# A recurrent attention block with a gated feed-forward network: late values of segments 58 to 61 kept in DRAM from step 1, an eighth early gate/up pair, two down loads in step 63

## The chip, the core and the metric

One core of one Trainium2 chip runs the whole program. Its engines run their own instruction streams side by side: TensorE (PE; its weight loads are listed as PEld), VectorE (DVE), ScalarE (ACT), GpSimd (POOL) and SyncE (SP), which here mostly issues DMAs. They wait for each other by semaphores. The metric is the device time of one execution in microseconds (us); the time of the kernel before is the median of three runs. Besides there is one profiled execution with a trace of every instruction.

## The reference

All inputs are bf16: 2048 rows of width 640, 32 heads of 128, 64 segments of 32 rows, a memory of 8 rows, and a feed-forward width of 1728.

```python
def _A_ref(x, mem0, Wq, Wk, Wv, Wo, seg_len):
    ...
    mem = mem0
    for s in range(n_seg):
        xs = x[:, s * seg_len:(s + 1) * seg_len, :].copy()
        h = jnp.concatenate([mem, xs], axis=1)
        q = jnp.einsum('btd,dhe->bhte', h, Wq)
        ...
        scores = jnp.where(mask[None, None], scores, -1000000000.0)
        p = _softmax(scores, axis=-1)
        o = jnp.einsum('bhqk,bhke->bhqe', p, v)
        o = jnp.einsum('bhte,hed->btd', o, Wo)
        mem = o[:, :M, :].copy()
        outs.append(o[:, M:, :])
...
h = x + _A_ref(_layernorm(x, axis=-1), A_mem0, A_Wq, A_Wk, A_Wv, A_Wo, A_seg_len)
h2 = h + _B_ref(_layernorm(h, axis=-1), B_W_gate, B_W_up, B_W_down)
```

`_B_ref` is relu(x Wgate) times (x Wup), times Wdown. The first eight output rows of a segment are the memory of the next, so the 64 segments form a chain.

## The kernel before

**Steps.** Step s (0 to 63) handles the memory and the first 24 rows of segment s: K, Q and V projections (`project`, L387 and L414), scores (L510), the memory rows' product with the values (`pv_mem`, L564), the output projection (`wo_split` L629, `wo_pass` L612), and from that the memory rows of the next segment (`to_act_split`, L656 and L658), with which step s+1 begins. The product for the other rows of segment s-1 (`pv_x`, L707) runs inside step s, and reads merged values from VM, which SP copies there.

**Late rows.** The last eight rows of a segment don't depend on the memory. Those of four segments are projected together, 32 rows at a time: `act_e[p]` holds them, and `extra_units` gives three steps of each group of four one of the K, Q and V products (40 matmuls of 512 columns), cut in three parts (`filler(0)` to `filler(2)`) that stand between the parts of the recurrence in PE's order. Results go to Ke, Qe and Ve, two buffers each; those of buffer 1 are parts of `ends`. Step 1 has no such unit.

**Early products.** Near the end some of these places are used otherwise. The late K and Q of segments 54 to 61 are made before step 1 and kept in DRAM (`next_d`). The units freed so compute gate/up pairs of the first 512 rows of the feed-forward part (`early_product`, steps 50, 51, 54, 55, 58, 59 and 60, L913), whose inputs lie in the unused halves of Ke, Qe and Ve; results go to `hx_d` in DRAM. NE = 7 counts them. Step 56 still projects the values of segments 58 to 61, after which the feed-forward input in buffer 0 is overwritten by the saved K and Q.

**Fills.** `fill_of(s)` says how many extra weight loads or halved matmuls K, Q and V of step s are given. They change no result: a matmul that could reuse the loaded weights loads them again, or a matmul of 512 columns is made as two of 256.

**Feed-forward part.** In step 63 and behind it, `gate_up(0, j)` computes the remaining pairs of block 0, the first four with 32-column groups (L913), the others full width (L1023), the last as a tail from Wt (L1036); `down_pair` follows (L1325), then blocks 1 to 3. Weights are loaded into the space of the projection weights: `load_piece` takes the next of the pieces of Wg and Wu, `load_down(n)` three row chunks of Wd once the K weights are no longer used.

**Order.** Every operation is added to one list. Each engine takes its operations in the order of the list, and waits are derived from the named keys that operations read and write. DMAs on SP are issued in that order too, so a DMA that waits holds those behind it.

Of the kernel before, what the change touches and what calls it, by code (L numbers as in the profile page):

```python
# [5 lines left out]
BF16 = mybir.dt.bfloat16  # L6
# [21 lines left out]
class _Graph:  # L28
# [10 lines left out]
    def add(self, eng, fn, r=(), w=(), dma=False):  # L39
        if eng == "pool" and not dma:  # L40
            r, w = tuple(r) + (("pool",),), tuple(w) + (("pool",),)
        op = _Op(eng, fn, tuple(r), tuple(w), dma)
        self.ops.append(op)
        return op
# [133 lines left out]
def build_kernel(nc, A_x, A_mem0, A_Wq, A_Wk, A_Wv, A_Wo, A_seg_len, B_W_gate, B_W_up, B_W_down, out):  # L178
    _, S, D = A_x.shape
    M = A_mem0.shape[1]  # L180
    _, H, Dh = A_Wq.shape
# [17 lines left out]
    xn2_d = nc.dram_tensor("xn2_d", [128, DC, 2 * TB], BF16)  # L199
    attn_d = nc.dram_tensor("attn_d", [S, 4, DC * 32], BF16)  # L200
    ends_d = nc.dram_tensor("ends_d", [128, 64 * H + 8 * VW], BF16)
    NE = 7
    next_d = [nc.dram_tensor(f"next{i}_d", [128, 32 * H], BF16) for i in range(4)]
    hx_d = nc.dram_tensor("hx_d", [128, NE, TB], BF16)

    es = ExitStack()
# [78 lines left out]
    def ap(t, off, dims, p0=0, n=128):  # L285
        if isinstance(t, _Part):
            t, off = t.whole, t.off + off
        row = 1
        for s in t.shape[1:]:
            row *= s  # L290
        return bass.AP(t, p0 * row + off, [[row, n]] + dims)
# [59 lines left out]
    def dma(dst, src, r=(), w=(), eng="sp"):  # L351
        add(eng, lambda e: e.dma_start(dst, src), r=r, w=w, dma=True)  # L352
# [123 lines left out]
    def chunks_of(flat):  # L476
        return flat.rearrange("p (c t) -> p c t", t=128)

    def place(s):
        if s < 2 or s >= NSEG - 2:  # L480
            return 1, s % 4
        return (s - 2) // 4 % 2, (s - 2) % 4
# [106 lines left out]
    def flip_ox(s, halves=(0, 1)):  # L589
        p = (s + 1) % 2  # L590
        for kh in halves:
            add("dve", lambda v, kh=kh: v.transpose(ap(oT[p], 160 * kh + M, [[320, 4], [40, 4], [1, 32]]),  # L592
                                                       ap(tox, 128 * kh, [[256, 4], [1, 4], [4, 32]])),
                r=[("ox", kh, t) for t in range(2)], w=[("oT", p, "x", kh)])
# [337 lines left out]
        j = EARLY_STEPS.index(s)  # L932
        dma(chunks_of(t[:, :]), src[:, 128 * j:128 * j + 128].rearrange("(c p) f -> p c f", p=128), w=[k])

    EARLY_STEPS = (NSEG - 14, NSEG - 13, NSEG - 10, NSEG - 9, NSEG - 6, NSEG - 5, NSEG - 4)

    def early_product(s):
        n, hp = EARLY_STEPS.index(s), 1 - place(s)[0]
# [20 lines left out]
    def extra_units(s):  # L959
        p, r = 1 - place(s)[0], place(s)[1]  # L960
        if s == NSEG - 3:
            p = 1 - place(NSEG - 1)[0]
            j = 0
            a, ks = act_e[p], [("acte", p)]
        elif 2 <= s < NSEG - 3 and r < 3:
            j = (1, 0, 2)[r]
            a, ks = act_e[p], [("acte", p)]
            if s in EARLY_STEPS:
                return early_product(s)
        else:  # L970
            return None, None

        def part(n):
            for c, halves in PARTS[n]:
                project(a, ks, j, halves, [BQ[i] for i in halves], (c,))

        def evac():
            for i in range(2):
                if j == 2:
                    to_v(BQ[i], Ve[p], i, ("Ve", p), "act")  # L980
                else:
                    to_tok(BQ[i], 2 + i, "act")
            for i in range(2):
                if s == NSEG - 3:
                    flip(2 + i, Qe[p], i, [("Qe", p, i)])
                elif j < 2:
                    flip(2 + i, (Qe, Ke)[j][p], i, [(("Qe", "Ke")[j], p, i)])
        return part, evac

    EARLY = tuple(range(15, 47, 4))  # L990

# [128 lines left out]
    FILL = (56, 39, 7, 52)  # L1120

    def fill_of(s):
        n = {1: 31, 2: 8, 50: 0, 51: 25, 54: 0, 55: 25, 57: 39, 58: 0, 59: 27, 60: 40, 61: 39, 62: 50, 63: 0}.get(s, FILL[s % 4])
        alone = min(n // 4, 3)
        rest = n - 4 * alone
        return [k < 3 - alone for k in range(3)], [2 * ((rest // 2 + k) // 4) + (k == 0 and rest % 2) for k in range(4)]

    for s in range(1, NSEG):
# [11 lines left out]
        def filler(n):  # L1140
            if units:
                units(n)
            if woe:
                woe_pass(BQ[0], WPARTS[n])
        if s > 0:
            a, ks = pass_act(s)
            held, parts = fill_of(s)
            if s in (NSEG - 14, NSEG - 13, NSEG - 10, NSEG - 9, NSEG - 5, NSEG - 4):
                early_weights(s, 1)
            elif s in (NSEG - 12, NSEG - 8):  # L1150
                q = 1 - place(s)[0]
                for n in range(2):
                    dma((ends[:, 1024 * n:1024 * n + 1024] if q else (Ke, Qe)[n][0][:].rearrange("p h t -> p (h t)")),
                        next_d[2 * q + n][:, :], r=[("next", 2 * q + n)] + [("next", 3, i) for i in range(2) if q * n],
                        w=[(("Ke", "Qe")[n], q, i) for i in range(2)])
                add("pool", lambda p, q=q: p.memset(ap(Ve[q], Dh, [[VW, 8], [1, VW - Dh]]), 1.0),
                    w=[("Ve1", q), ("Ve", q, 0), ("Ve", q, 1)])
            elif s == NSEG - 3:
                for n in range(2):
                    dma(ends[:, 1024 * n:1024 * n + 1024], ends_d[:, 1024 * n:1024 * n + 1024], r=[("ends",)],  # L1160
                        w=END_KEYS[2 * n:2 * n + 2])
            elif s == 1:
                dma(ends_d[:, :], ends[:, :], r=END_KEYS, w=[("ends",)])
                far_save(0)
                far_save(1)
# [27 lines left out]
            if not last:  # L1193
                for i in range(2):
                    project(a, ks, 0, (i,), ((P0, P1)[i],), *WAYS[i], held=i == 1 and held[1], parts=parts[2 + i])
                    to_tok((P0, P1)[i], 2 + i, "act")
                    flip(2 + i, Qo, i, [("Qo", i)])
                    if i == 0:
                        norm_x_late(0)
                        flip_ox(s - 1, (0,))  # L1200
            else:
                norm_x_late(0)
                flip_ox(s - 1, (0,))
            if s == NSEG - 2:
                for n, (lo, hi) in enumerate(((0, 1), (1, 2), (2, 3), (3, DC))):
                    dma(xn2T[0][:, lo:hi, :], xn2_d[:, lo:hi, 0:TB], r=[("xn2_d", u) for u in range(4)] + [("Wdone", 0)],
                        w=[("xn2", 0, n)])
# [56 lines left out]
        if s in (NSEG - 15, NSEG - 11, NSEG - 7):  # L1264
            early_rows(1 - place(s + 1)[0], 0, 2)
            early_rows(1 - place(s + 1)[0], 4, DC)
            if s == NSEG - 7:
                early_weights(s + 1, 1)
        elif s in (NSEG - 14, NSEG - 10, NSEG - 6, NSEG - 5):
            early_weights(s + 1, 0)  # L1270
        norm_mem(s, 1)
        flip_mem(s, 1)
# [4 lines left out]
                w=[("Qo", i) for i in range(2)])  # L1277
        if s > 0 and not woe and s != NSEG - 3:
            late_o(s - 1)
        if s % 4 == 1 and ln:  # L1280
            ln1_back(nb, chunks_of(at[:, :]), [("at",)], "pool")
        mask_x(s)
        if e2c is not None:
# [8 lines left out]
        if s >= 1:  # L1292
            rows_split(P3, P1, wtok, ("wtok",))
            store_attn(wtok, ("wtok",), M, 32 * (s - 1), RID)
        filler(2)
        if woe:
            for n in ((s - 2, s - 1) if s == NSEG - 2 else (s - 1,)):
                late_o(n)
# [79 lines left out]
            down_store(b, u + q, o[q])  # L1378


    def load_down(n):
        lo, hi = 3 * n, min(3 * n + 3, FC - 1)
        r = [("Wdone", 1)]
        dma(Wd[:, lo:hi, :], B_W_down[128 * lo:128 * hi, :].rearrange("(j p) d -> p j d", p=128), r=r, w=[("Wd", n)])
        if n == 4:
            for q in range(2):
                dma(Wd[FR * q:FR * q + FR, FC - 1, :], B_W_down[FM:F, :], r=r, w=[("Wd", 5 + q)])

    def load_rows(b, r):
        dma(h_rows[b][:, :, :], h_d[TB * b:TB * b + TB, :].rearrange("(u p) d -> p u d", p=128),  # L1390
            r=[("h_d", 4 * b + u) for u in range(4)] + r, w=[("h", b, u) for u in range(4)])
# [18 lines left out]
        load_piece(("Wdone", 0))  # L1410
    rows(P3, s % 2, s - 1)
    gate_up(0, NE + 1)
    for n in range(2):
        load_down(n)
    pv_x(s, P0)
    norm_x(P0)
    norm_x_late(P0)
# [21 lines left out]
    for b in range(NBLK):  # L1439
        if 0 < b < NBLK - 1:  # L1440
            for u in range(4):
                ln2_load(4 * (b + 1) + u)
        for j in range(FC):
            p = j - NE if b == 0 else j
            if b or p > 3:
                gate_up(b, j)
            if b == 0 and p == 5:
                load_rows(0, [("Wdone", 1), ("hT", 0, j)])
            if b == 0 and p in (5, 6):
                load_piece(("hT", 0, j - 1))  # L1450
                load_piece(("hT", 0, j - 1))
            if 0 < b < NBLK - 1:
                fronts, backs = (1, 3, 5, 7), (3, 5, 7, 9)
                if p in fronts:
                    ln2_front(4 * (b + 1) + fronts.index(p))
                if p in backs:
                    ln2_back(4 * (b + 1) + backs.index(p), None)
        if b == 0:
            load_rows(1, [("Wdone", 2), ("hT", 0, FC - 1)])
        assert not pieces  # L1460
        for n in range(2):
            down_pair(b, n)
# [63 lines left out]
```

## Time and profile before

| what | value |
|---|---|
| median of three runs | 980.47 us (979.86 to 980.51) |
| profiled execution | 980.59 us, its span 978.9 us |
| PE busy | 955.6 us (98%), 26159 matmuls |
| PE weight loads | 537.1 us (55%), 24953 |
| VectorE busy | 726.3 us (74%) |
| ScalarE busy | 522.5 us (53%) |
| GpSimd busy | 187.4 us (19%) |
| DMA | 85.74 MB, mean 88 GB/s |

A timeline row gives the start in us, the length in us, the engine, the source line, the operation, the tile written and the tiles read, shapes, a count where rows of one kind were merged, and in brackets how long the engine had been idle before and what released it. PE's matmuls overlap, so a row's length is not its cost: that is read from the distance of starts. The row of a stage (us from A to B) gives busy time and count for each engine, the granted PE clock, the busy share of the DMA engines and GB/s.

### The profile page before, as it was taken

To read this page: it belongs to the slowest core of one execution; us is meant where nothing else is said; L and a number is where in the kernel's file an instruction comes from. 1 tells how busy PE (TensorE), PEld (TensorE's weight loads), DVE (VectorE), ACT (ScalarE), POOL (GpSimd) and SP (SyncE) were. 2 spreads that over 40 slices of the span, in tenths; PEclk is the share of its full clock that TensorE was granted. 3 is DMA by queue.
4 is the path that set the end of the run, shared out by engine and by line. 5 is a ranking of instruction groups with operands and counts; after the bars stand their busy time and mean duration, and the time that the engine had idled before them with its cause. 6 is when DMAs were issued, how large, how long until landed. Compare 5 with 4: busy or idle time off the path is not lost.

```text
span 978.9 us, 56745 instructions
## 1 busy us (share of the span) xinstructions
PE 955.6 (98%) x26159; PEld 537.1 (55%) x24953; DVE 726.3 (74%) x2041; ACT 522.5 (53%) x1326; POOL 187.4 (19%) x428
## 2 busy tenths in 40 slices
PE   4989999999999999999999999999999999999998
PEld 1346565656555656555656566565666565444443
DVE  3668888888888888888888888887878873445232
ACT  1466666666666666666666666666655552122120
POOL 7021112121313131313131313020201110000000
PEclk9999999999999999999999999999999999999999
DMA  9951111121232223223231323142323348503000
GB/s 360 417 209 40 43 40 46 37 55 49 54 63 54 64 56 68 58 62 60 57 61 55 62 57 61 40 107 64 104 62 100 76 120 278 185 21 95 21 14 28
DMA packets 89845, 85.74 MB, mean 88 GB/s; under 512 B 52283, under 2 KB 75011, under 8 KB 87683
## 3 DMA queue, kind: packets, MB, share of 16 engines
q1 hardware_dynamic: 87872, 81.15, 29.2%
q8 instruction: 201, 3.29, 1.4%
q10 hardware_dynamic: 1730, 0.96, 0.4%
q14 instruction: 42, 0.34, 0.1%
HBM read 45.33 MB, written 10.62 MB: 57 GB/s over the span
## 4 chain that ended last, share of the span: by engine, by line
PE 93%; SPq 3%; DMA 2%; DVE 1%; issue 0%; ACT 0%; POOL 0%; DVEq 0%; ACTq 0%; POOLq 0%
PE ps L414 46%; PE ps L1023 9%; PE ps L612 7%; PE ps L387 7%; PE ps L629 7%; PE ps L678 4%; SPq L352 3%; PE ps L1325 3%; PE ps L913 2%; PE ps L510 2%; PE ps L707 2%; DMA Wo<-in_A_Wo_dram 2%; PE ps L564 2%; PE ps L1036 0%; PE ps L1338 0%
## 5 line engine op out<-in xcount | busy, mean ns | idle before, releaser
L414 PE MATMUL ps<-W,act_r 128*32 128x512 bf16 (+1 forms) x8383 | 461.9, 358 | 1.0 <-DVE act_r L658 0.6
L414 PEld LDWEIGHTS ps<-W,act_r 128*32 128x32 bf16 x8383 | 220.0, 96 | 162.5 <-DVE act_r L658 21.5
L438 ACT ACTIVATE tok<-ps 128x512 bf16<-128x512 f32 x182 | 105.2, 594 | 59.0 <-PE ps L414 48.0
L438 ACT ACTIVATE tox<-ps 128x512 bf16<-128x512 f32 x138 | 81.8, 598 | 59.5 <-PE ps L414 49.1
L433 DVE STREAM_TRANSPOSE Ko<-tox 128x512 bf16<-128x512 bf16 x128 | 89.1, 697 | 30.6 <-ACT tox L438 29.9
L414 PE MATMUL ps<-W,act_e 128*32 128x512 bf16 x1056 | 101.7, 384 | 3.2 <-DVE TBf L491 2.0
L592 DVE STREAM_TRANSPOSE oT<-tox 128x512 bf16<-128x512 bf16 x128 | 95.8, 748 | 0.0
L433 DVE STREAM_TRANSPOSE Qo<-tok 128x512 bf16<-128x512 bf16 x124 | 85.7, 691 | 0.9
L612 PE MATMUL ps<-Wo,oT 128*32 128x160 bf16 x4032 | 81.7, 233 | 2.7 <-DMA Wo<-in_A_Wo_dram 2.3
L629 PE MATMUL ps<-Wo,oT 128*32 128x320 bf16 x2016 | 79.9, 299 | 0.3 <-issue 0.3
L612 PEld LDWEIGHTS ps<-Wo,oT 128*32 128x32 bf16 x4032 | 70.4, 97 | 13.0 <-DMA Wo<-in_A_Wo_dram 3.2
L438 ACT ACTIVATE Vp<-ps 128x512 bf16<-128x512 f32 x127 | 75.2, 592 | 0.5 <-ACT Vp L438 0.5
L387 PE MATMUL ps<-W,act_e 128*32 128x512 bf16 x744 | 73.5, 386 | 0.0
L1051 ACT ACTIVATE g<-ps 128x512 bf16<-128x512 f32 x45 | 26.1, 593 | 79.6 <-PE ps L1023 78.1
L645 ACT ACTIVATE SA<-TA 64x40 f32<-64x40 f32 x126 | 29.6, 235 | 65.3 <-DVE TA L642 64.5
L526 ACT ACTIVATE Pm<-ps 128x64 bf16<-128x64 f32 x126 | 28.2, 224 | 66.8 <-PE ps L510 66.7
L586 DVE STREAM_TRANSPOSE oT<-om 128x128 bf16<-128x128 bf16 x126 | 39.2, 311 | 31.0 <-ACT om L578 30.9
L510 PE MATMUL ps<-Qo,Ko 128*32 128x40 bf16 x2048 | 60.9, 181 | 0.0
L629 PEld LDWEIGHTS ps<-Wo,oT 128*32 128x32 bf16 x2016 | 50.5, 96 | 18.4 <-DVE rm L576 0.8
L510 PEld LDWEIGHTS ps<-Qo,Ko 128*32 128x32 bf16 x2048 | 46.4, 94 | 25.3 <-DVE Qo L433 17.9
L1052 DVE TENSOR_TENSOR hT<-g,ps 128x512 bf16<-128x512 bf16 x45 | 30.8, 687 | 39.2 <-PE ps L1023 35.2
L518 POOL COPY Qo<-ends 128x256 bf16<-128x256 bf16 x32 | 14.3, 446 | 232.1 <-DVE oT L586 214.6
(159 smaller groups left out, 1528.2 us busy)
## 6 DMA issues: line engine op xcount, KB each, us to landing
VM<-Vp SPq DMA_DIRECT2D x126, 65.0 KB
VM<-Vp SPq DMA_DIRECT2D x63, 130.0 KB
W<-in_A_Wk_dram SPq DMA_DIRECT2D x5, 1024.0 KB
W<-in_A_Wq_dram SPq DMA_DIRECT2D x5, 1024.0 KB
W<-in_A_Wv_dram SPq DMA_DIRECT2D x5, 1024.0 KB
Wo<-in_A_Wo_dram SPq DMA_DIRECT2D x8, 640.0 KB
attn_d<-wtok SPq DMA_DIRECT2D x248, 7.5 KB
xt<-in_A_x_dram SPq DMA_DIRECT2D x16, 160.0 KB
```

The source lines that it names most:

```text
L387: return pe.add_instruction(mybir.InstMatmult(name=nc.get_next_instruction_name(), engine=mybir.EngineType.PE, ins=[pe.lower_ap(rhs), pe.l ...
L414: ins = pe.matmul(*b, start=(c == ends[0]), stop=(c == ends[1]), skip_group_check=True)
L433: add("dve", lambda v: v.transpose(dst[:, 16 * i:16 * i + 16, 0:32], tok[t][:, :].rearrange("p (h f) -> p h f", f=32)), r=tok_keys(t), w=keys)
L438: add("act", lambda a: a.activation(dst, src, ACTF.Copy), r=r, w=w)
L510: i = pe.matmul(bank((P0, P1)[hf])[q:q + 32, o:o + 40], (Ko if a == 0 else Ke[p])[:, h, :], Qo[:, h, :], start=True, stop=True, skip_group ...
L586: add("dve", lambda v: v.transpose(ap(oT[par], 160 * hf, [[40, 4], [320, 4], [1, 8]]), ap(om, 128 * hf, [[1, 4], [4, 32]])), r=[("om", hf) ...
L592: add("dve", lambda v, kh=kh: v.transpose(ap(oT[p], 160 * kh + M, [[320, 4], [40, 4], [1, 32]]), ap(tox, 128 * kh, [[256, 4], [1, 4], [4, ...
L612: i = pe.matmul(bank(bk)[32 * gg:32 * gg + 32, 0:160], src[:, hb, 0:32], w[:, gg], start=(hb == CH[16 * halves[0]]), stop=(hb == CH[-1]), ...
L629: i = pe.matmul(bank(bk)[32 * q:32 * q + 32, 0:320], src[:, hb, 0:32], w, start=(n == 0), stop=(n == 7), skip_group_check=True)
L678: ins = pe.matmul(bank(bk)[32 * q:32 * q + 32, 0:320], src[:, hb, 0:32], w[:, 2 * (q % 2):2 * (q % 2) + 2], start=(i == 0), stop=(i == 15) ...
L1023: ins = pe.matmul(bank(bk), w[:, c, lo:lo + 128], xn2T[par][:, c, :], start=(c == 0), stop=(c == DC - 1))
L1052: add("dve", lambda v: v.tensor_tensor(hT[par][:, j, :], g1[gi][:, :], bank(bu), ALU.mult), r=[B(bu), ("g1", gi)], w=[("hT", par, j)])
```

## The change

The values of the late rows of segments 58 to 61 are projected in step 1 by the same 40 matmuls that step 56 had, into Ve[1], and step 2 stores that tile in `nextv_d`. Step 57 loads them into Ve[0], with the saved K and Q, whose loads were in step 56. The copies out of `at` that refill the projection's input (`ln1_back`) stand behind the new product in step 1. Step 56 becomes an early step: NE is 8, the early pairs are columns 0 to 1023, and the feed-forward part starts its own with pair 8. The fills of steps 1, 2, 3 and 56 change. The first two calls of `load_down` move into step 63, behind the first half of the previous segment's transposes.

```diff
-    NE = 7
+    NE = 8
+    nextv_d = nc.dram_tensor("nextv_d", [128, 8 * VW], BF16)
...
-    EARLY_STEPS = (NSEG - 14, NSEG - 13, NSEG - 10, NSEG - 9, NSEG - 6, NSEG - 5, NSEG - 4)
+    EARLY_STEPS = (NSEG - 14, NSEG - 13, NSEG - 10, NSEG - 9, NSEG - 8, NSEG - 6, NSEG - 5, NSEG - 4)
...
+        elif s == 1:
+            p, j, a, ks = 1, 2, a2, k2
...
-        n = {1: 31, 2: 8, 50: 0, 51: 25, 54: 0, 55: 25, 57: 39, 58: 0, 59: 27, 60: 40, 61: 39, 62: 50, 63: 0}.get(s, FILL[s % 4])
+        n = {1: 0, 2: 0, 3: 26, 56: 40, 50: 0, 51: 25, 54: 0, 55: 25, 57: 39, 58: 0, 59: 27, 60: 40, 61: 39, 62: 50, 63: 0}.get(s, FILL[s % 4])
...
-            elif s in (NSEG - 12, NSEG - 8):
+            elif s == NSEG - 12:
...
+            elif s == NSEG - 7:
+                for n in (1, 0):
+                    dma((Ke, Qe)[n][0][:].rearrange("p h t -> p (h t)"), next_d[n][:, :], r=[("next", n)],
+                        w=[(("Ke", "Qe")[n], 0, i) for i in range(2)])
+                dma(ap(Ve[0], 0, [[1, 8 * VW]]), nextv_d[:, :], r=[("nextv",)], w=[("Ve1", 0), ("Ve", 0, 0), ("Ve", 0, 1)])
+            elif s == 2:
+                dma(nextv_d[:, :], ap(Ve[1], 0, [[1, 8 * VW]]), r=[("Ve1", 1), ("Ve", 1, 0), ("Ve", 1, 1)], w=[("nextv",)])
...
             else:
                 norm_x_late(0)
                 flip_ox(s - 1, (0,))
+                for n in range(2):
+                    load_down(n)
...
-        elif s in (NSEG - 14, NSEG - 10, NSEG - 6, NSEG - 5):
+        elif s in (NSEG - 14, NSEG - 10, NSEG - 9, NSEG - 6, NSEG - 5):
             early_weights(s + 1, 0)
...
-        if s % 4 == 1 and ln:
+        if s % 4 == 1 and s > 1 and ln:
             ln1_back(nb, chunks_of(at[:, :]), [("at",)], "pool")
...
         filler(2)
+        if s == 1:
+            ln1_back(nb, chunks_of(at[:, :]), [("at",)], "pool")
...
     gate_up(0, NE + 1)
-    for n in range(2):
-        load_down(n)
```

More of the change, by code (lines that the diff above doesn't have):

```diff
@@ L988, in extra_units, with load_down @@
         return part, evac
+    def load_down(n):
+        lo, hi = 3 * n, min(3 * n + 3, FC - 1)
+        r = [("Wdone", 1)]
+        dma(Wd[:, lo:hi, :], B_W_down[128 * lo:128 * hi, :].rearrange("(j p) d -> p j d", p=128), r=r, w=[("Wd", n)])
+        if n == 4:
+            for q in range(2):
+                dma(Wd[FR * q:FR * q + FR, FC - 1, :], B_W_down[FM:F, :], r=r, w=[("Wd", 5 + q)])
     EARLY = tuple(range(15, 47, 4))
@@ L1147, in build_kernel @@
             held, parts = fill_of(s)
-            if s in (NSEG - 14, NSEG - 13, NSEG - 10, NSEG - 9, NSEG - 5, NSEG - 4):
+            if s in (NSEG - 14, NSEG - 13, NSEG - 10, NSEG - 9, NSEG - 8, NSEG - 5, NSEG - 4):
                 early_weights(s, 1)
-            elif s in (NSEG - 12, NSEG - 8):
-                q = 1 - place(s)[0]
+            elif s == NSEG - 12:
                 for n in range(2):
[L1153 to L1157, printed above, removed]
+                    dma(ends[:, 1024 * n:1024 * n + 1024], next_d[2 + n][:, :],
+                        r=[("next", 2 + n)] + [("next", 3, i) for i in range(2) if n],
+                        w=[(("Ke", "Qe")[n], 1, i) for i in range(2)])
+                add("pool", lambda p: p.memset(ap(Ve[1], Dh, [[VW, 8], [1, VW - Dh]]), 1.0),
+                    w=[("Ve1", 1), ("Ve", 1, 0), ("Ve", 1, 1)])
+            elif s == NSEG - 7:
[5 more added lines that the diff above has]
+                dma(nextv_d[:, :], ap(Ve[1], 0, [[1, 8 * VW]]), r=[("Ve1", 1), ("Ve", 1, 0), ("Ve", 1, 1)], w=[("nextv",)])
             elif s == NSEG - 3:
@@ L1378, in down_pair @@
             down_store(b, u + q, o[q])
[L1381 to L1387, printed above, removed]
     def load_rows(b, r):
@@ L1446, in build_kernel @@
                 gate_up(b, j)
-            if b == 0 and p == 5:
+            if b == 0 and j == FC - 2:
                 load_rows(0, [("Wdone", 1), ("hT", 0, j)])
-            if b == 0 and p in (5, 6):
+            if b == 0 and j >= FC - 2:
                 load_piece(("hT", 0, j - 1))
```

## The prediction

> **What bounds the kernel now.** First the page: its head, the chain that ended last, the clock row. Then the PE rows of steps 1 and 2 side by side, the same rows of steps 54, 56 and 60, and the feed-forward stage from 805 us on.
>
> ```profile
> span 978.9 us, 56745 instructions
> PE 93%; SPq 3%; DMA 2%; DVE 1%; issue 0%; ACT 0%; POOL 0%; DVEq 0%; ACTq 0%; POOLq 0%
> PEclk9999999999999999999999999999999999999999
> ```
>
> TensorE (PE) carries 93% of the chain at full granted clock, so matmul time that leaves PE's own order leaves the end, and matmul time that is added costs as much as it doesn't fit into a PE gap. Gaps exist only where the recurrence makes PE wait. Step 1 has two; step 2, which runs 40 extra matmuls (L414 on act_e), has none:
>
> ```profile
> 65.55 0.22 PE L564 MATMUL ps<-ends,Pbd 128*32 128x129 bf16 x4
> 66.64 0.24 PE L564 MATMUL ps<-ends,Pbd 128*32 128x129 bf16 x4 [0.81 <-DVE Pbd L532]
> 69.99 1.26 PE L414 MATMUL ps<-W,act_r 128*32 128x512 bf16 x20 [0.61 <-DVE act_r L658]
> ...
> 72.30 0.24 PEld L707 LDWEIGHTS ps<-VM,Px 64*32 64x32 bf16 x32 [0.47 <-DMA VM<-Vp]
> 77.39 0.23 PE L564 MATMUL ps<-Ve,Pbd 128*32 128x129 bf16 x4
> 78.58 0.23 PE L564 MATMUL ps<-Ve,Pbd 128*32 128x129 bf16 x4
> 81.96 1.25 PE L414 MATMUL ps<-W,act_r 128*32 128x512 bf16 x25
> ```
>
> L707 is the product of the previous segment's rows, the first L564 the start of the memory rows' values, and the L414 rows at 69.99 and 81.96 begin steps 2 and 3. From the first L564 to the next step's first matmul step 1 takes 69.99 - 65.55 = 4.44 us without extra matmuls, step 2 takes 81.96 - 77.39 = 4.57 us with 40. So 40 matmuls behind this recurrence cost 0.13 us, not their own length.
>
> Their own length, where PE waits for nothing, is in the feed-forward stage: one gate/up pair reaches from the first to the second of these rows.
>
> ```profile
> 821.45 1.25 PE L1023 MATMUL ps<-xn2T,Wg 128*128 128x512 bf16 x5
> 823.62 1.24 PE L1023 MATMUL ps<-xn2T,Wg 128*128 128x512 bf16 x5
> ```
>
> 823.62 - 821.45 = 2.17 us for ten matmuls.
>
> **The change part by part.** *The eighth pair.* The listing of the changed program has one block of five Wg and five Wu full-width matmuls fewer in block 0, everything behind it unchanged and following without a gap: **-2.17 us**.
>
> *Step 56.* It exchanges 40 V matmuls for 40 gate/up matmuls. Step 60 does this product already:
>
> ```profile
> 723.42 0.39 PE L414 MATMUL ps<-W,act_e 128*32 128x512 bf16 x4
> 727.89 0.39 PE L414 MATMUL ps<-W,act_r 128*32 128x512 bf16 x4
> ...
> 771.37 1.25 PE L913 MATMUL ps<-ends,xt 128*32 128x512 bf16 x20
> 775.83 0.39 PE L414 MATMUL ps<-W,act_r 128*32 128x512 bf16 x4
> ```
>
> From the start of the extra work to the next step: 4.47 us in step 56, 4.46 us in step 60. **0**, and the bounds are -0.05 and +0.1. Behind it ACT does one 0.6 us pass instead of two, VectorE one more of 0.69 us ahead of the Ko transposes; steps 51, 55 and 61 start with the same.
>
> *Step 1.* 40 V matmuls go where step 2 has its 40. **+0.13 us** by the two differences above. Part of it returns: the L707 of step 2 comes 72.30 - 69.99 = 2.31 us after the step's start, that of step 3 (row below) 84.23 - 81.96 = 2.27 us; step 2's was released by its VM load, 0.04 us later than the other, and when step 2 starts 0.13 us later that load is in time: **-0.04 us**. Bounds: 0 if all hides, and +2.17 - 0.81 - 0.61 = +0.75 if only the two gaps are filled one to one. I take the value of step 2, which has the same matmuls in the same places. ACT gains two copies into Ve[1] at the place where every V step has them. POOL's eight copies out of `at` begin with the first row below and ended at 71.57; now they wait for the last V matmul at about 70.1 and end near 72.6, before POOL's next work and five us before step 2's extra matmuls, behind its first L564 at 77.39, read what they fill:
>
> ```profile
> 69.13 1.33 POOL L460 COPY act_r<-at 128x120 bf16<-128x120 bf16 x4
> 70.52 1.05 POOL L460 COPY act_e<-at 128x40 bf16<-128x40 bf16 x4
> 73.73 2.50 POOL L370 TENSOR_SCALAR xl<-xl,mv,rs 128x640 bf16<-128x640 bf16 x1 [2.16 <-ACT rs L363]
> ```
>
> **0**; without that cover each us of theirs would hold step 2's extra matmuls, and PE behind them, by one.
>
> *Fill counts (31, 8, 52, 56 to 0, 0, 26, 40).* They add weight loads and cut matmuls in two. Step 54 runs with none, step 3 with 52:
>
> ```profile
> 84.23 0.42 PE L707 MATMUL ps<-VM,Px 64*32 64x129 bf16 x32
> 87.72 0.38 PE L414 MATMUL ps<-W,act_r 128*32 128x512 bf16 x4
> ...
> 703.97 0.62 PE L414 MATMUL ps<-W,act_r 128*32 128x512 bf16 x9
> 706.24 0.42 PE L707 MATMUL ps<-VM,Px 64*32 64x129 bf16 x32
> 709.74 0.38 PE L414 MATMUL ps<-W,act_r 128*32 128x512 bf16 x4
> ```
>
> Start to L707: 2.27 us in both. L707 to the last value matmuls of the first half: 3.49 (52) against 3.50 (none). So fills cost **0**. What they do is in the listings: with a matmul that loads weights counted as two, four steps have 3072 PE instructions, 12 x 256, and the change keeps that grid: steps 1 to 3 have 678 + 721 + 766 = 2165 before and 711 + 714 + 740 = 2165 after, step 56 has 769 in both. Only inside steps 1 to 3 do instructions shift against it, by up to 33.
>
> ```profile
> q8 instruction: 201, 3.29, 1.4%
> 798.29 1.21 PE L612 MATMUL ps<-Wo,oT 128*32 128x160 bf16 x57 [0.25 <-issue]
> ```
>
> 3.29 MB in 201 packets is 16.4 KB, 256 instructions of 64 bytes each. The second row is the one place after step 0 where PE stopped for nothing that the profile shows, in the densest stretch of step 62. I take 0 for the shifted steps and keep 0.25 us for each as the upper bound. The Trainium skill (Runtime: NRT & Kernel Launch, "Instruction fetch mechanics") says that instructions are refilled in 16 KiB blocks and that crossing one is mostly hidden; the packet size agrees, and by the rule alone shifting against the grid would cost nothing.
>
> *SP's queue.* Step 2 gains one store (nextv_d, 260 KB). It waits for ACT's copies of step 1's values, early in step 2, and the VM loads behind it move by one issue (some 0.4 us); they are read by the L707 at 84.23. **0**. Step 56 gives two loads to step 57 (Qe, Ke), with a third (Ve) that waits for the hx_d store of step 56. Queued behind it on SP is the transpose into `at`:
>
> ```profile
> 719.24 1.40 SPq L352 DMA_DIRECT2D Qe<-next_d  x1
> 730.33 1.90 SPq L375 DMA_TRANSPOSE at<-xl  x1
> 738.45 0.64 POOL L460 COPY act_r<-at 128x120 bf16<-128x120 bf16 x2
> ```
>
> One issue of 1.40 us and two shorter ones from 730.33 on reach 732.5; the store's landing, 2 us by estimate (one 1.90 us row as the nearest length), falls inside that. The transpose then starts near 733 and ends its issue near 735, over 3 us before POOL reads `at` at 738.45. **0**; a delay beyond 3 us would stop POOL, which feeds the next step's late queries.
>
> *The down loads and the smaller weight pieces.*
>
> ```profile
> 806.18 0.37 ACTq L352 DMA_DIRECT2D Wu<-in_B_W_up_dram  x1
> 812.05 0.93 SPq L352 DMA_DIRECT2D Wd<-in_B_W_down_dram  x2
> 812.27 0.42 PE L707 MATMUL ps<-VM,Px 64*32 64x129 bf16 x32
> 816.24 5.97 SPq L352 DMA_DIRECT2D Wd<-in_B_W_down_dram  x4
> 822.68 1.04 POOL L1428 COPY Wt<-Wt 128x320 bf16<-128x320 bf16 x2 [6.61 <-DMA Wt<-in_B_W_gate_dram]
> 825.77 1.26 PE L1036 MATMUL ps<-xn2T,Wt 128*128 128x256 bf16 x10
> 804.00:808.00 4.00, 4.00 (x126) 2.22 (x116) 2.43 (x5) 2.58 (x6) 0.40 (x1) 1.00 0.51 118
> 812.00:824.00 12.00, 12.00 (x260) 6.87 (x253) 5.56 (x11) 3.28 (x7) 1.31 (x3) 1.00 0.96 313
> ```
>
> The last two rows end with DMA share and GB/s: 0.96 busy in 812 to 824, 0.51 in 804 to 808. The tail matmuls at 825.77 move to 823.60, and POOL's copies that feed them end at 823.72. Left as they were the loads would take 0.1 to 0.3 us back. But two down loads (960 KB) go to about 804, the third weight pieces shrink by 320 KB and hx grows by 128 KB: 1152 KB less ahead of Wt, which at 313 GB/s is some 3.8 us. **0**, with +0.3 as bound.
>
> **Sum.** -2.17 + 0.13 - 0.04 = -2.08 us. Against the profiled execution (980.59 us around its span of 978.9) 978.5; that execution stands 0.12 above the median of 980.47, so I predict **978.4 us** as median, 0.21% less. About 0.2%, 1.96 us, is what a measurement tells from no change, so the forecast lies only just beyond it.
>
> **The rivals.** *Steps 1 to 3 cost more.* For: instructions shift against the grid just there, and a stall has a row. Against: steps 1 to 5 begin at different places of the grid (offsets 200, 110, 63, 61, 62) with no stall in their rows. Price 0.25 us in each of steps 1 and 2, or 0.75 for the unit: about 979.0.
>
> *The end is held by loads.* For: 0.96 DMA share. Against: the bytes moved ahead. Price 0.3 us: 978.7.
>
> *More than the pair.* For: the gaps of step 1 are wider, 1.42 us together, than the 0.13 that is left over in step 2 lets expect. If its V work hides fully and step 56 gains its bound, 0.13 + 0.05: 978.2. Against: step 2 shows the excess with the same matmuls.
>
> *Slower.* The 960 KB of down weights stand in SP's queue ahead of VM's loads and beside the two 320 KB pieces that ACT issues in step 63, the second at 806.18. VM must land by 812.27, and PE takes everything behind L707 in order. About 1.6 MB and 0.27 MB at 313 GB/s from 804 end near 810.2, 2 us early; at the 118 GB/s of the quieter row, near 820, and L707 would wait some 8 us. Each us past 812.27 costs one; it decides against the change once VM lands after 814.35, and at 815.5 the time is 981.6. For it: nothing in SP's order keeps VM ahead. Against: 118 is what was asked for at 0.51 share, not what could be had. The Trainium skill (DMA: Bandwidth & Descriptors, "Issuing engines are not separate DMA queues") says that DMAs of all issuers run on the same 16 engines and interleave, so that ACT's pieces are no second road; by it alone the wait is possible, and no row here decides it.
>
> **How the numbers follow.** Forecast 0.62 (978.4; its own range 978.0 to 978.8, since the runs of before spread over 0.65 us), of which I give 0.52 to faster and 0.10 to the same. Costlier first steps 0.15 and loads 0.06: the same. More than the pair 0.10: faster. Slower mechanism 0.07. Faster 0.62, same 0.31, slower 0.07. Range 977.7 to 979.7: it takes in the first three rivals.
>
> **What would show it.** Step 1 from first L564 to the next step near 4.57 us with the 0.81 and 0.61 gaps gone; step 56 unchanged within 0.1 us; the tails about 2.1 us earlier than 825.77, POOL's Wt copies ending earlier than that by over 1 us; L707 of step 63 without a wait. Wrong would be: an "issue" gap in steps 1 to 3, L707 released by VM's DMA, or a transpose into `at` that POOL waits for in step 57.

## The result: 2.7 us slower, and the profile after

The changed kernel takes 983.18 us as the median of 9 runs (982.08 to 986.51), the kernel before 980.51 us on the same chip (9 runs, 979.86 to 982.14): ratio 1.0027, 95% interval 1.0016 to 1.0038. Forecast was 978.4. The profiled execution took 983.14 us around a span of 981.4; the granted clock is full.

```profile
span 981.4 us, 56722 instructions
PE 93%; SPq 3%; DMA 3%; issue 1%; POOL 0%; DVE 0%; POOLq 0%
q8 instruction: 201, 3.29, 1.4%
```

These are the head, the chain that ended last and the instruction queue of the page of after. "issue" on the chain, time in which an engine waited for nothing that the profile names, was 0% and is 1%, both rounded. The rows below show which of it stands on TensorE (PE). Line numbers of after are one higher than before's up to L914; L1023, L1036, L1325 and L1428 become L1034, L1047, L1346 and L1439.

To find where time is lost, take the start of each step (VectorE's product into `act_r`, L658 before, L659 after) from both traces:

```
step            1       2       3      57      58      63
before      57.95   69.76   81.64  727.57  739.56  799.85
after       57.87   69.73   81.65  727.23  740.24  800.34
```

From step 1 to step 57 nothing is lost: after is 0.08 ahead at step 1 and 0.34 at step 57. Some 0.3 of it is gained at the end of step 34, where VectorE idles 0.34 us ahead of `act_r` in before. This isn't chance: the other four traces of before's order of PE work (e2, e6, e8, e13) take as long there, and the eight of the changed one take 0.3 less. Why stays open. Step 57 takes 13.01 us instead of 11.99 (+1.02). The rest is in step 63 and behind it. Here are PE's rows of step 57, and those of SP and POOL, from the timeline of after (start, duration, what; the bracket is idle time in front and its releaser):

```profile
737.47 0.32 PE L613 MATMUL ps<-Wo,oT 128*32 128x160 bf16 x6
738.66 1.22 PE L613 MATMUL ps<-Wo,oT 128*32 128x160 bf16 x58 [0.87 <-issue]
...
731.56 0.43 SPq L353 DMA_DIRECT2D Ke<-next_d  x1
732.74 0.32 SPq L353 DMA_DIRECT2D Ve<-nextv_d  x1
733.11 1.26 SPq L376 DMA_TRANSPOSE at<-xl  x1
...
738.47 0.64 POOL L461 COPY act_r<-at 128x120 bf16<-128x120 bf16 x2 [0.49 <-DMA at<-xl]
```

PE stops in the middle of one pass of 64 equal matmuls that read the same two tiles, and the profile names nothing that it waited for. SP's queue ran as forecast: the transpose into `at` was issued by 734.37. But POOL, which reads what it brings, waited 0.49 us for it and began at 738.47: it landed about 4 us after its issue. No row of PE waits for that copy. The 16 DMA engines were full just then: the last two columns of a window's row are their busy share (packets count where they start, so it can pass 1) and GB/s. Here are two rows of after and one of e4, a run below without the stop:

```profile
734.00:736.00 2.00, 2.00 (x91) 1.29 (x82) 1.96 (x9) 1.43 (x5) 0.00 (x0) 1.00 1.02 200
736.00:738.00 2.00, 1.79 (x60) 1.12 (x50) 1.36 (x7) 0.79 (x3) 0.45 (x1) 1.00 1.00 240
...
734.00:736.00 2.00, 2.00 (x100) 1.51 (x100) 1.81 (x9) 1.34 (x5) 0.00 (x0) 1.00 0.40 90
```

The end of the recurrence, same view of after; by the forecast PE's work here should have come 2.17 us earlier. The last row is before's, from where the passes of L678 (L679 in after) begin:

```profile
804.48 0.98 SPq L353 DMA_DIRECT2D Wd<-in_B_W_down_dram  x2
807.60 1.84 SPq L353 DMA_DIRECT2D VM<-Vp  x3
...
814.22 0.42 PE L708 MATMUL ps<-VM,Px 64*32 64x129 bf16 x32 [1.11 <-DMA VM<-Vp]
...
817.82 0.82 PE L914 MATMUL ps<-xn2T,Wu 128*32 128x512 bf16 x12
820.59 0.61 PE L914 MATMUL ps<-xn2T,Wu 128*32 128x512 bf16 x8 [1.95 <-issue]
821.03 2.35 PE L679 MATMUL ps<-Wo,oT 128*32 128x320 bf16 x64
825.43 0.46 PE L679 MATMUL ps<-Wo,oTe 128*32 128x320 bf16 x8 [0.15 <-issue]
826.05 1.03 PE L1034 MATMUL ps<-xn2T,Wg 128*128 128x512 bf16 x4 [0.16 <-issue]
827.99 1.25 PE L1047 MATMUL ps<-xn2T,Wt 128*128 128x256 bf16 x10
...
816.95 2.35 PE L678 MATMUL ps<-Wo,oT 128*32 128x320 bf16 x64
```

Count from the start of step 63. VM's matmuls begin 13.88 us after it (814.22 - 800.34) where before had 12.42: +1.46. From there to the first L679 of the last passes are 6.81 us instead of 4.68: +2.13, a stop behind the 12th of 20 equal Wu matmuls. From L679 to the first full-width pair it is 5.02 instead of 4.50. But the Wg row at 826.05 has four of the pair's five matmuls: the first one's record is missing, so its "issue" of 0.16 is no wait. A block of five takes 1.08 us, and Wu begins at 826.91, so the pair began near 825.83: 4.80, or +0.30. Together +3.89. With 0.49 from the steps ahead, -2.17 for the pair that is gone and 0.28 from the tails to the end (153.41 instead of 153.13), this is the 2.5 us by which the spans differ. The DMA engines in these stretches:

```profile
804.00:808.00 4.00, 4.00 (x127) 2.11 (x119) 2.76 (x6) 2.29 (x6) 0.40 (x1) 1.00 0.79 212
808.00:812.00 4.00, 3.93 (x125) 2.76 (x112) 1.50 (x3) 1.11 (x3) 0.00 (x0) 1.00 0.94 285
812.00:816.00 4.00, 2.89 (x83) 1.35 (x75) 1.92 (x5) 0.83 (x2) 0.00 (x0) 1.00 0.98 292
816.00:820.00 4.00, 2.64 (x52) 1.06 (x40) 1.91 (x4) 1.58 (x4) 0.40 (x1) 1.00 1.08 342
```

804 to 808 was 0.51 before and is 0.79: the two down loads are now issued at 804.48 instead of 812.05, just ahead of VM.

**What stands at the stops.** Number PE's instructions in the order of the built program, a matmul that loads its own weights as two. The long stops of after stand at 44738 (7th matmul of the pass in step 57) and 49602 (13th of the fourth grouped Wu), a short one at 49858 (57th of the last oTe pass); the 0.25 us of before, quoted in the prediction, at 48578. All four leave 194 when divided by 256, and 256 instructions are one packet of the instruction queue q8. Narrow windows of the DMA view give the packets' starts to 0.2 us. PE crosses the block end ahead of 49602 near 811.6; that packet starts at 818.0, and PE goes on at 820.59. In step 57 the packet starts at 736.2, and PE goes on at 738.66. In a quiet step a packet starts within a microsecond of the crossing (in step 24 of before, crossings near 335.3, 339.4 and 343.2, packets at 336.2, 340.4 and 344.0) and then has the time of 256 instructions to arrive. So the theory for the experiments: PE holds one block ahead, its refill goes over the same 16 DMA engines as data, and when these are full it comes too late.

### The profile page after: what moved, and what is told of

It is laid out like the page before. It is cut to its first block, busy times and chain, and to the rows that moved or that the text cites. A ratio compares the mean times of both kernels' runs of the same rounds, so it can differ in the third digit from the quotient of the medians.

```text
span 981.4 us, 56722 instructions
## 1 busy us (share of the span) xinstructions
PE 952.9 (97%) x26145; PEld 535.0 (55%) x24933; DVE 726.5 (74%) x2041; ACT 523.0 (53%) x1326; POOL 187.8 (19%) x427
## 4 chain that ended last, share of the span: by engine, by line
PE 93%; SPq 3%; DMA 3%; issue 1%; POOL 0%; DVE 0%; POOLq 0%
PE ps L415 47%; PE ps L1034 9%; PE ps L613 7%; PE ps L388 7%; PE ps L630 7%; PE ps L679 4%; SPq L353 3%; PE ps L1346 3%; PE ps L914 2%; PE ps L511 2%; PE ps L708 2%; DMA Wo<-in_A_Wo_dram 2%; PE ps L565 1%; DMA VM<-Vp 1%; PE ps L1047 0%
## 5 line engine op out<-in xcount | busy, mean ns | idle before, releaser
L415 PE MATMUL ps<-W,act_e 128*32 128x512 bf16 x1032 | 99.0, 382 | 4.4 <-DMA W<-in_A_Wq_dram 1.7
L388 PE MATMUL ps<-W,act_e 128*32 128x512 bf16 x728 | 71.6, 383 | 0.0
```

Of the source, the lines that this page charges most:

```text
L388: return pe.add_instruction(mybir.InstMatmult(name=nc.get_next_instruction_name(), engine=mybir.EngineType.PE, ins=[pe.lower_ap(rhs), pe.l ...
L415: ins = pe.matmul(*b, start=(c == ends[0]), stop=(c == ends[1]), skip_group_check=True)
```

## The experiments

Each ratio is against runs of the kernel before on the same chip at the same time (980.45 us for e1 to e10, 980.73 for e11 to e13). Their intervals reach some 0.9 us to either side, 1.1 for e13 and 1.4 for e2.

**e1: the two down loads back at their old place; all else of the change stays.**

```
# after norm_x_late(0), flip_ox(s - 1, (0,)) of step 63
-                for n in range(2):
-                    load_down(n)
# after gate_up(0, NE + 1)
+    for n in range(2):
+        load_down(n)
```

> The changed kernel with the first two down loads back behind the ninth gate/up pair, all else kept. Theory A (the moved down loads cost the end: they hold the values of VM that the product of step 63 waits for, and they hold the refill of PE's instructions): the wait on VM in step 63 (1.11 us) and the stop of 1.95 us in the last Wu block of the grouped pairs go, about 4.1 us in all, and the time is 979.0 (978.7 to 979.6). Theory B (the eighth pair itself, its shorter cover or its larger hx load, costs the end): the time stays between 982.5 and 983.5.

980.08 us, ratio 0.9999 [0.9991, 1.0008]: some 3 us won back by moving two loads. VM's matmuls wait for nothing and the 1.95 us stop is gone. The time is 1.1 above the 979.0 that I expected. The timeline of e1 shows a wait that the expectation didn't have:

```profile
812.28 0.42 PE L708 MATMUL ps<-VM,Px 64*32 64x129 bf16 x32
...
824.60 1.04 POOL L1439 COPY Wt<-Wt 128x320 bf16<-128x320 bf16 x2 [8.52 <-DMA Wt<-in_B_W_gate_dram]
825.78 1.25 PE L1047 MATMUL ps<-xn2T,Wt 128*128 128x256 bf16 x10 [2.04 <-POOL Wt L1439]
```

The tail matmuls, 2.17 us earlier in PE's order, wait 2.04 us for their weights. With the loads in their old order the pair's gain is taken back there.

**e2: the kernel before with only the down loads moved** to where the change has them (the reverse of the edit above).

> The kernel before with only the first two down loads moved into step 63. Theory A: the same two losses appear without the eighth pair, 984.6 (983.5 to 985.2). Theory B: nothing moves, 980.5 within 0.5.

984.13 us, ratio 1.0038 [1.0024, 1.0052]. The move alone costs 3.7 us, with the same marks in the same places, seen in the timeline of e2:

```profile
813.31 0.42 PE L707 MATMUL ps<-VM,Px 64*32 64x129 bf16 x32 [0.44 <-DMA VM<-Vp]
...
816.91 0.82 PE L913 MATMUL ps<-xn2T,Wu 128*32 128x512 bf16 x12
820.23 0.62 PE L913 MATMUL ps<-xn2T,Wu 128*32 128x512 bf16 x8 [2.50 <-issue]
```

Again 12 matmuls, the stop, 8 matmuls. The data wait is the small part. A further stop of 0.36 us, at 811.39, is at the block end before, 49346.

**e4: e1, and the Ke and Ve loads of step 57 at the end of that step's list** (only Qe stays early).

```
-                for n in (1, 0):
-                    dma((Ke, Qe)[n][0][:]..., next_d[n][:, :], ...)
-                dma(ap(Ve[0], 0, [[1, 8 * VW]]), nextv_d[:, :], ...)
+                dma(Qe[0][:]..., next_d[1][:, :], ...)
...
                 early_weights(s + 1, 1)
+                dma(Ke[0][:]..., next_d[0][:, :], ...)
+                dma(ap(Ve[0], 0, [[1, 8 * VW]]), nextv_d[:, :], ...)
```

> The changed kernel with the down loads back and with the loads of Ke and Ve in step 57 put behind that step's other loads, so that only Qe is loaded early in step 57. Theory A for step 57 as well (three loads early in the step hold a refill of instructions, and PE stops 0.87 us in the output projection): the stop goes, step 57 takes 12.0 us again, and the time is 978.1 (977.8 to 978.6), faster than the kernel before by about 2.4. Rival for step 57 (the early product of step 56 or its evacuation is what delays step 57): the stop stays and the time is that of the kernel with only the down loads back, 979.0.

979.48 us, ratio 0.9992 [0.9984, 1.0001]. The stop in step 57 is gone (the step takes 11.90 us instead of 13.01, and its pass runs as one row of 64), but the median came down by 0.6 only, less than these runs can tell from zero or from a full microsecond, and is 1.4 above the 978.1 expected. In the profiled executions the whole gain arrives (979.33 against 980.93, the tails 1.61 us earlier); what stands against 978.1 there is the tails' wait of 1.72:

```profile
736.96 1.29 PE L613 MATMUL ps<-Wo,oT 128*32 128x160 bf16 x64
...
824.17 1.25 PE L1047 MATMUL ps<-xn2T,Wt 128*128 128x256 bf16 x10 [1.72 <-POOL Wt L1438]
```

**e5: after with the fill count of step 62 at 18 instead of 50**, which puts every later PE instruction 32 places earlier in the listing (`62: 50` becomes `62: 18`). Block ends then fall behind the 13th matmul of another Wu group (49346) and behind the 8th of the oT pass (49602).

> The changed kernel with fill 18 in place of 50 in step 62, so that all PE instructions from step 62's Q products on stand 32 places earlier in the stream. Theory of refills (PE stops where a block of 256 instructions ends; counted from the listing all stops stand at place 194 of 256): the long stop moves from behind the 12th matmul of the fourth grouped Wu block to behind the 8th matmul of the row product of step 63 (L679, oT) that follows, and is still 1 to 2.5 us. Rival (the Wu weights are late): the stop stays behind the 12th Wu matmul. Time 983 within 1 us under both.

One run, 984.12 us. From its timeline:

```profile
813.35 1.03 PE L914 MATMUL ps<-xn2T,Wu 128*32 128x512 bf16 x13
816.18 0.61 PE L914 MATMUL ps<-xn2T,Wu 128*32 128x512 bf16 x7 [1.80 <-issue]
...
821.40 0.45 PE L679 MATMUL ps<-Wo,oT 128*32 128x320 bf16 x8
822.60 2.08 PE L679 MATMUL ps<-Wo,oT 128*32 128x320 bf16 x56 [0.75 <-issue]
```

The stop no longer stands behind the 12th Wu matmul; both stops went with the block ends. The same trace has three more, all at block ends: 1.25 us at 44738, 0.64 at 48578 and 0.27 at 48834. The place is confirmed, the size at 49602 missed: 0.75 instead of 1 to 2.5 us, perhaps because the longer stop came one block earlier. The time is just outside the 982 to 984 expected.

**e6 and e13: 1.9 MB that nobody needs, in the kernel before.** Four copies of 480 KB from the down weights to a spare DRAM tensor, in step 24. The outputs are computed as before.

```
+    spare_d = nc.dram_tensor("spare_d", [128, 12, D], BF16)
...
+                if s == 24 and i == 0:
+                    for n in range(4):
+                        dma(spare_d[:, 3 * n:3 * n + 3, :], B_W_down[384 * n:384 * n + 384, :]..., 
+                            r=[("Wdone", 1)], w=[("spare", n)])    # e13: without r
```

> The kernel before with four copies of 480 KB, DRAM to DRAM, that nobody waits for, issued by SP in step 24 after its K projection. Theory of the instruction refill: PE stops with nothing that the trace shows it waiting for ('issue') directly ahead of the 15th matmul of that step's wo_pass (near 355 us, the next block end of PE's listing behind the start of the copies) or at the block end after it, the first matmuls of pv_x near 359 us, 0.3 to 2.5 us long; 980.8 to 984. Rival, only data come late: no such 'issue' stop; a stop stands ahead of matmuls that read VM and is put down to the DMA VM<-Vp, or there is none (980.5).

991.99 us, and no answer. The copies read the mark ("Wdone", 1), which the next projection writes, so PE waited 9.31 us for the copies themselves, which says nothing of instructions. The times in that expectation also belong to step 25; step 24 runs from 332.6 to 344.6. e13 drops the mark.

> The kernel before with the four spare copies of 480 KB of the run before, now without any tie to PE's work (there the copies read a mark that the next projection writes, so PE waited 9.31 us for them, which tells nothing of instructions). SP issues them behind the attn_d stores of step 24, about 335 us; block ends of PE's listing in that step are at the 2nd matmul of pv_x (335.3), the 9th of 16 projection matmuls among the scores (339.4), the 15th of wo_pass (343.2), and in step 25 at the first of pv_x (347.2). Theory of the instruction refill: an 'issue' stop at exactly 339.4 or 343.2, 0.3 to 5 us long in all; total 980.8 to 985. Rival, only data come late: no 'issue' stop; at most a wait for VM at 347.2, put down to its DMA; 980.5 or what that wait is.

984.72 us, ratio 1.0034 [1.0022, 1.0045]. From the timeline and the windows of e13:

```profile
342.50 0.45 PE L613 MATMUL ps<-Wo,oT 128*32 128x160 bf16 x14
345.48 1.08 PE L613 MATMUL ps<-Wo,oT 128*32 128x160 bf16 x50 [2.54 <-issue]
...
349.51 0.42 PE L708 MATMUL ps<-VM,Px 64*32 64x129 bf16 x32
...
824.92 0.46 PE L679 MATMUL ps<-Wo,oTe 128*32 128x320 bf16 x8 [1.32 <-issue]
```

```profile
338.00:340.00 2.00, 2.00 (x108) 1.12 (x100) 2.00 (x6) 1.06 (x3) 0.00 (x0) 1.00 0.88 266
340.00:342.00 2.00, 2.00 (x64) 0.99 (x48) 1.44 (x7) 1.58 (x5) 0.00 (x0) 1.00 1.00 341
342.00:344.00 2.00, 0.94 (x34) 0.57 (x26) 1.20 (x4) 0.87 (x5) 1.11 (x3) 1.00 1.00 352
344.00:346.00 2.00, 0.52 (x32) 0.52 (x36) 0.00 (x0) 0.24 (x1) 0.00 (x0) 1.00 0.26 88
```

Fourteen matmuls, 2.54 us of nothing, then the 15th: the block end that had been named. The packet that PE needed starts at 342.8, 3.8 us after the crossing near 339.0, while the engines are 0.88 to 1.00 busy, and PE goes on 2.7 us after its start. VM's matmuls follow without a wait, so late data are not what stopped PE. (The fourth row is a second stop, far away at 49858, where the profiled execution of before had none: the length of these stops differs from execution to execution.)

**e7, e8, e10: the tails' weights first.** Since e4 lost 1.72 us to Wt behind three Wd loads and hT in SP's queue, e7 is e4 with the two Wt loads and POOL's copies put ahead of row pass 62 and of every Wd and hT load. e8 does this to the kernel before; e10 is e7 with Ke and Ve early again, as the change has them.

```
     for _ in range(2):
         load_piece(("Wdone", 0))
+    for q, src in enumerate((B_W_gate, B_W_up)):
+        dma(Wt[:, 0, :, ...], src[:, FM:F]..., r=[("Wdone", 0)], w=[("Wt", q, 0)])
+        add("pool", ...)
     rows(P3, s % 2, s - 1)
```

> The kernel with both undone (down loads back, Ke and Ve of step 57 late), and the two Wt loads with their two copies on POOL put ahead of row pass 62's stores and of all Wd and hT loads. Theory: what is left of that kernel's loss is one wait, 1.72 us of the tails for Wt, which stands behind three Wd loads and hT in SP's queue; with Wt ahead the wait is gone and nothing takes its place: 979.48 - 1.72 = 977.8 us (977.3 to 978.3), ratio 0.997, the first tail directly behind the third full-width block of 5 matmuls x 2. Rival: the 16 DMA engines are full from 816 to 824 and the same bytes still pass, so another wait takes its place (VM, or PE's instructions): 979.0 to 980.5.

> The kernel before with nothing but the Wt loads and copies moved ahead in the same way. Theory: there the copies end at 823.72 and the first tail runs at 825.77, so no wait is there to win: 980.5 us, the same within 0.1%. Rival, slower: 160 KB more in the queues around 811 us bring the next PE instructions late and PE stops before its next block end: 980.8 to 982.

> The kernel of e7 with Ke and Ve of step 57 early again, as the change has them: the only difference from e7. Theory: the stop inside step 57's wo_pass (1.0 us, PE without its next instructions) stands in the path and nothing hides it now: e7 + 1.0 = 978.8 us (978.4 to 979.3). Rival: it is taken up later as in the pair of kernels with Wt late, where the same difference was 0.6 us: 978.4 or less.

e7: 980.14 us, 0.9996 [0.9987, 1.0006]; e8: 980.43, 1.0001 [0.9992, 1.0010], as expected; e10: 980.49, 1.0003 [0.9994, 1.0012]. My theory of e7 (977.8) fell, and its rival held: the tails run without a wait, and the next consumer of the loads waits instead. The timeline of e7, and its windows:

```profile
823.75 1.26 PE L1047 MATMUL ps<-xn2T,Wt 128*128 128x256 bf16 x10
826.44 0.30 PE L1343 MATMUL ps<-Wd,hT 128*128 128x320 bf16 x1 [1.43 <-DVE hT L1057]
```

```profile
812.00:816.00 4.00, 4.00 (x104) 1.88 (x100) 3.38 (x7) 1.31 (x4) 1.07 (x3) 1.00 0.55 86
816.00:820.00 4.00, 4.00 (x116) 2.77 (x108) 1.04 (x2) 1.03 (x2) 0.25 (x1) 1.00 1.05 406
```

The first down matmul waits 1.43 us. The profile names VectorE's product of the tails, but in e4 the down matmuls ran on directly behind the tails without it; of what that matmul needs, the down loads and hT are left, and the engines were at 1.03 or more from 816 to 828. Which of these loads came last the trace doesn't say. (This execution also lost 0.83 us in step 54, whose code is that of e4, 0.31 of it at a block end.) e10 differs from e7 by 0.35 us, less than these runs can tell; its stop in step 57 was only 0.19 us in the profiled execution. (The 978.8 expected was built on e7's 977.8.) What Ke and Ve cost in the median is therefore between nothing and 1 us, and I leave it there.

**e11: e7 with the first two down loads ahead of row pass 62's stores.** In e7's window from 812 to 816 the engines were half idle; SP waited for that pass's result until 813.29 and issued the first Wd load at 814.06.

```
         add("pool", ...)
+    for n in range(2):
+        load_down(n)
     rows(P3, s % 2, s - 1)
     gate_up(0, NE + 1)
-    for n in range(2):
-        load_down(n)
```

> e7 with the first two down loads put behind the Wt loads and ahead of row pass 62's stores. In e7 SP waits from 812.9 to 813.3 us for that pass's result and sends nothing else, and the 16 DMA engines are busy only 0.55 of 812 to 816 us (86 GB/s) and 1.03 to 1.09 from 816 to 828; the first down matmul then waits 1.43 us. Theory: what holds the end is when the last of these loads lands, and the idle 0.45 x 4 us (some 1.8 us of all engines) in front is what can be won: the wait of 1.43 us goes, 980.14 - 1.4 = 978.7 us (978.2 to 979.3). Rival: 960 KB more around 811 us bring PE's next instructions late, an 'issue' stop of 0.5 to 2 us ahead of the 13th Wu matmul of the fourth grouped pair or the 57th of the last oTe pass: 979.2 to 981.

979.50 us against 980.73, ratio 0.9985 [0.9976, 0.9993]: faster than both kernels, by 1.2 us against before, though 0.8 above my 978.7 and outside its range. Against e7 the gain is too small for these runs to tell. No instruction stop showed in step 63 (the rival), and the wait ahead of the down matmuls shrank from 1.43 to 0.83 us:

```profile
820.10 1.25 PE L1034 MATMUL ps<-xn2T,Wg 128*128 128x512 bf16 x5
821.19 1.24 PE L1034 MATMUL ps<-xn2T,Wu 128*128 128x512 bf16 x5
822.26 1.25 PE L1047 MATMUL ps<-xn2T,Wt 128*128 128x256 bf16 x10
824.35 0.30 PE L1343 MATMUL ps<-Wd,hT 128*128 128x320 bf16 x1 [0.83 <-issue]
```

This "issue" isn't at a block end (49914 leaves 250), so it isn't an instruction stop by the rule above; what it waited for stays open.

**e12: the change with only its two down loads moved, from ahead of VM to behind VM** and the last two gate/up pieces, ahead of row pass 62.

> The change with only the place of its two down loads altered: 4 us later in SP's queue, behind the VM loads and the last two gate/up pieces of step 63 instead of ahead of them. Theory (the loss of 3.1 us is their place): the VM wait (1.11 us) is gone, and the stop of 1.95 us at the 13th Wu matmul shrinks to under 0.5; the tails' wait for Wt of the kernel with the loads at their old place (2.04 us) shrinks too, to 1 or less: 979.0 us (978.4 to 980.0). Rival: the bytes are the same and the stop only moves (a stop of 1 us or more at the 13th Wu or the 57th oTe matmul): 981 to 983.

979.86 us, ratio 0.9989 [0.9980, 0.9998], inside the expected range. The two loads are issued at 811.57 instead of 804.48, and that is worth 3.3 us of time: no wait for VM, no stop in step 63, and 0.20 us left of the tails' wait. The stops of the early Ke and Ve loads are still there, at two block ends in a row (0.62 us in the pass of step 57, 0.65 behind the third matmul of step 58's VM product).

## Why the prediction was wrong, step by step

*The eighth pair, -2.17: right.* First full-width matmul to tails takes 822.26 - 820.10 = 2.16 us in e11, 4.32 before (825.77 - 821.45).

*Step 1, +0.13, and step 2's VM, -0.04: right.* The timeline of after:

```profile
65.47 0.23 PE L565 MATMUL ps<-ends,Pbd 128*32 128x129 bf16 x4
66.66 0.23 PE L565 MATMUL ps<-ends,Pbd 128*32 128x129 bf16 x4
70.05 1.25 PE L415 MATMUL ps<-W,act_r 128*32 128x512 bf16 x20
...
72.31 0.42 PE L708 MATMUL ps<-VM,Px 64*32 64x129 bf16 x32
```

70.05 - 65.47 = 4.58 us against 4.57 forecast, both gaps gone; 72.31 - 70.05 = 2.26. Step 56 takes 11.92 us (11.96 before), the fills show no cost, and steps 1 to 3 have no "issue" gap. The part of the change that looked most intricate went as worked out.

*SP's queue, 0: wrong.* The step asked only when each load's consumer needs its data. By that question it was nearly right; the transpose's 3 us of slack was used up whole, since its landing was taken for its issue. What it never asked is what else the engines carry at that time: with the early loads they were full (1.02 busy from 734 to 736), the refill came late, and PE stopped for 0.87 us in step 57. All five traces with Ke and Ve early (after, e1, e5, e10, e12) show that packet 1.2 to 2.0 us behind the crossing and a stop; in the other eight it starts within 0.4 us and nothing stops. Without the two loads ahead of it the transpose goes out sooner too (731.40 in e4, 733.11 in after), so whether their bytes or the transpose's later packets held the refill isn't separated.

*The down loads, 0 with +0.3 as bound: wrong, and the largest miss.* Moving them cost 3.1 us (983.18 against 980.08 of e1) and 3.7 us (e2 against before). About 1.1 us of it in after is the wait for VM of my slower rival, which got a chance of 0.07: what I argued against its 118 GB/s was that more could be had, but the 16 engines were already half busy there and the loads ahead of VM came first in the queue. The larger part, 1.95 us, no rival had: it is the wait for instructions at 49602. Of the three signs of being wrong that the prediction named, two showed: VM's DMA released that product in step 63, and POOL waited for the transpose in step 57.

*The stop of 0.25 us: read, counted, and put in the wrong place.* The prediction had the block size, the grid and a measured stop, and priced it for steps 1 to 3, where instructions shift against the grid. The shift cost nothing there; what costs is a refill under way while the engines are full. The row quoted there stood in step 62, where nothing shifts, and that was the hint. The Trainium skill (Runtime: NRT & Kernel Launch, "Instruction fetch mechanics") says that the cost of crossing a block is mostly hidden. The runs agree where the engines have room and disagree where they don't: 0.15 to 2.54 us per crossing.

*"The end is held by loads", 0.3: mis-sized.* I set the end of POOL's copies (823.72) against the tails' new place (823.60) and took the difference as the price. That holds only if the rest of PE's path stands still. With the stops undone PE comes earlier and the loads do not: 2.04 us in e1, 1.72 in e4. e7 shows that the order of the loads is not the cure by itself; with the first two down loads earlier, in e11, what is left of the wait is 0.83 us.

So the forecast's 2.08 us could be had only behind a road that I had counted as free: in after 3.89 us of stops and waits in step 63 and 1.02 in step 57 stand against them. How much of the 2.08 can be had is open. e11's profiled execution, with 0.83 us still waited, took 978.41 us, 2.2 less than before's (0.3 of that is step 34's), while its median is only 1.2 less. No trace of one of its slower executions shows where that microsecond goes.

## What to carry to other kernels

A load that nobody waits for still has a price when the DMA engines are near full: ask what else they carry at that moment, PE's own instructions included, and where PE's next block of 256 ends. When a load is moved forward in a queue, put it behind everything that is needed sooner, and check the stretch by its DMA share, not by its consumer alone. Here the same two loads cost some 3 us ahead of VM and nothing behind it (e12). When PE work is removed ahead of a stage that loads feed, work out when the last of its loads lands first; the gain ends there.

## What was unexpected in the hardware

PE's refill behaves as if it were asked for at one block end and needed at the next: stops stood at places that leave 194 modulo 256 in all nine traces that have such a stop, mostly within runs of equal matmuls. The refill packet started up to 6.4 us late (811.6 to 818.0) with the engines at 0.94 to 1.08.

The packet records of all 13 traces bear this out. From 60 to 830 us they have 2392 block ends with one refill packet since the block end before. PE crossed none of them sooner than 1.24 us after the end of that packet, and in all 18 stops it went on 1.24 to 1.54 us after it (2.3 to 3.0 us after its start, by the packet's length of 0.9 to 1.6 us). The eight packets that started over 2.5 us late all stood in stretches where the engines were at least 0.9 busy. What a late packet costs depends on the block: the one in step 57 takes 3.2 us when nothing stops, and a packet 1.75 us late stopped PE for 0.87. In before PE crosses 49858 without a stop, 2.5 us after its packet's start: nothing was to spare there, and in e13 the same place cost 1.32. Behind which data a late packet stood, no record shows.

The stop in step 57 was 0.87, 0.97, 1.25, 0.19 and 0.62 us long in after, e1, e5, e10 and e12, which share that code, so a single profile doesn't size it.
